# Loading the queries of later batches in two-token runs, so that the score matmuls read them in order

## The chip, the cores and the metric

The kernel runs on one core of one Trainium2 chip. The metric is the device time of one launch in microseconds (us). The kernel before took 751.44 us, the median of three runs that lie between 751.35 and 751.8 us.

## What is computed

For each of 4 batches and 8 heads (576 tokens of 64 numbers, 32 memory slots), a softmax of `phi` over the tokens condenses keys and values into 32 memory keys and 32 memory values. Each query token then attends to those 32 slots. The result, 2304 tokens of 512 numbers, goes through two feed-forward layers, the first with a leaky ReLU, the second with Mish. All data is float32.

```python
a = softmax(phi, over tokens)                          # (b, h, 576, 32)
k_m = einsum('bhsm,bhsd->bhmd', a, k);  v_m = einsum('bhsm,bhsd->bhmd', a, v)
scores = q @ k_m.T / 8                                 # (b, h, 576, 32)
x = softmax(scores, over the 32 slots) @ v_m           # heads side by side: (2304, 512)
h = x @ w_in;   x = maximum(0.01 * h, h) @ w_out       # (2304, 2048) and back
h = x @ w_in2;  out = (h * tanh(softplus(h))) @ w_out2
```

## The kernel before

Every large product is done as three products of TensorE's rounded float32 kind: an operand is split into a rounded part and the rest (`hi` and `lo` in the names). The memory values are first multiplied into `w_in` (`vw_tasks`, L927; matmuls on L947), so that the first layer is computed from the attention weights (`at_t`) directly. The first feed-forward network (`stage1`, L1187) walks over 128 units of 288 tokens by 128 hidden columns: six matmuls on L1198 make a hidden block, ScalarE (ACT) and VectorE (DVE) split it, and twelve matmuls on L1231 add it to four accumulators. Between these units stands the attention of the next batch. The second network (L1552 and L1705) follows.

The attention of batches 1 to 3 is `kv_rest` (L502) and `score_rest` (L676). A batch has two groups `g` of four heads, and each head has its own 32 partitions, so a group's queries fill 128 partitions. One DMA per group loads them: partition `p` of a head gets tokens 18p to 18p+17, one run of 18 tokens of 64 numbers (4,608 bytes). VectorE then transposes the tile in place in blocks of 32 by 32 (L695). After that a partition holds one of 32 features, and along the partition stand token-in-run (18), feature half (2) and partition of origin (32), in this order. Two score blocks follow, one for the even and one for the odd tokens. A block (L709 to L719, the row of its matmuls is L713) has 16 matmuls: two feature halves, four heads, two groups. Each takes 32 rows and gives 32 of the 128 output partitions, over 288 columns. Batch 1 keeps the two groups in two tiles (`qs_t`, `qT_t`), batches 2 and 3 in one (`kvq_t`). VectorE transposes the scores back (L724), the softmax runs over 32 slots, and a last transpose and a split give `at_t`. Batch 0 is done in another way (`score_tasks`, L811: transposes on TensorE, score matmuls on L864), which the change leaves alone.

In the profile a float32 matmul of the program appears as two records, so a score block is 32 records; a matmul on split operands is one.

All instructions are put in order at build time by a planner (`Order.run`, L94): a task has a priority, the engines that may do it with an assumed duration each, and the buffers that it takes. The planner steps through its own clock and places the ready task of lowest priority. SyncE (SP) issues all DMAs, in order, from one queue; an issue waits there until its buffer is free, and those behind it wait too. Where two engines may do a task, L115 takes the one that would end first, after adding a bias; the constant `TOP` is the bias on VectorE for one step (`top`, L371) of unpacking a weight tile (`decode`, L359): ScalarE does it on L374, VectorE on L376.

Of the kernel before, what the change touches and what calls it, by code (L numbers as in the profile page):

```python
# [23 lines left out]
def hop(a, b):  # L24
# [6 lines left out]
K = dict(  # L31
    LAG1=2, WIN=8, OB=2, RS=4, FILL=36, A1=10, S1=8.0,
    A2=30, S2=2.6, V1=2.4, V2=14, W2=56.0, W2S=3.8, O='phi0 kv0 phi1 q0 w0 kv1 q1 w1 w2 w3', HF0=-20.0, HF1=-7.0,
    HFD=0.3, TOP=0.3, HI=0.2, WO=2.0, WOL=1, WC=3.0, WC0=-38.0, V0=3.0, COLD=20, GL=1.5, AL=5.0, XL=22.0, T='0:1 0:1 1:2 0:2 1:2', SB=1,
    DW=280e3, DQ=1.3, DP=1.2, DS=0.78, DI=0.38, L4=0.5, L4P=1.6, L4S=0.8, L4T=5.0, MA=6, QL=4, PL=6, BH=(9,3,3,3,3), FK=-52.5, DWF=0.85, MV="......rvvrrvvrvr",
)

# [122 lines left out]
def kernel(  # L160
# [14 lines left out]
    M = phi.shape[3]  # L175
# [5 lines left out]
    HG = 4  # L181
# [11 lines left out]
    RQ = S // 32  # L193
# [83 lines left out]
    def dma(**args):  # L277
        sched.issued += 1
        nc.sync.dma_start(**args)
# [3 lines left out]
    def add(engines, prio, fn, deps=(), take=(), use=(), bias=None):  # L283
        t = sched.add(engines, prio, fn, deps, take, use, bias)
        for b in (*take, *use):
            if b.pool is spool:
                early.append(t)
            elif b.pool is rawpool:
                middle.append(t)
        return t  # L290


    def dve(n):
        return n / 960 + 0.065
# [4 lines left out]
    def act(n, ps=False):  # L299
        return n / 1196 + (0.051 if ps else 0.093)  # L300
# [4 lines left out]
    def mb(shape_bytes):  # L305
        return shape_bytes / K["DW"]
# [193 lines left out]
    RB = 9  # L500
# [175 lines left out]
    def score_rest(b, pq, ps, dp):  # L676
        qs = [q_s.new([P, RQ, 2, M]), qT_s.new([P, RQ, 2, M])] if b == 1 else [kvq.new([P, NG, RQ, 2, M])] * NG
        q_of = [lambda g=g: qs[g].t if b == 1 else qs[g].t[:, g] for g in range(NG)]
        parts, ld0 = [], None
        for g in range(NG):  # L680
            flat = lambda g=g: q_of[g]().rearrange("p r e i -> p (r e i)")
            new = b == 1 or not g

            def ld(e, g=g, new=new, flat=flat):
                if new:
                    qs[g].make()
                dma(out=flat(), in_=q[b, g * HG:(g + 1) * HG].rearrange("h (p r) d -> (h p) (r d)", r=RQ))

            ld0 = add(
                {"SP": K["DS"] * mb(589824)}, pq - K["QL"], ld, [] if new else [ld0], [qs[g]] if new else [], [] if new else [qs[g]],  # L690
            )
            if b == 1:
                ld0.behind = w_loads[1][K["BH"][3 + g]:][:1]
            parts.append(add(
                {"DVE": dve(1152) + 0.1}, pq + 0.7 * g, lambda e, flat=flat: nc.vector.transpose(out=flat(), in_=flat()), [ld0], (), [qs[g]],  # L695
            ))
        kb = kT[b, 0][0]
        a = [at_tag.new([P, 2, S], F32R) for _ in range(NG)]
        ab = [[], []]
        for hf in range(2):  # L700
            ps0 = ps[hf]
            T = T_tag.new([P, NG, RB, M])
            pss = [misc.new([P, NB1]) for _ in range(NG)]

            def fsc(e, hf=hf, T=T, pss=pss):
                T.make()
                for x in pss:
                    x.make()
                for y in range(2):  # L709
                    for h in range(HG):  # L710
                        for g in range(NG):
                            rows, o = slice(M * h, M * (h + 1)), M * (h ^ g)
                            nc.tensor.matmul(  # L713
                                out=pss[g].t[o:o + M, :].rearrange("p (i r) -> p i r", i=M),
                                lhsT=kb.t[rows, g, y, :],
                                rhs=q_of[g]()[rows].rearrange("p (r u) e i -> p u e i r", u=2)[:, hf, y],
                                start=(y == 0),
                                stop=(y == 1),
                            )  # L719

            ts = add({"PE": 1.2}, ps0, fsc, [*parts, *kT[b, 0][1], *kT[b, 1][1]], [T, *pss], [*qs[:1 + (b == 1)], kb])
            tt = [add(
                {"DVE": dve(NB1)}, ps0 + 0.2,
                lambda e, g=g, T=T, pss=pss: nc.vector.transpose(out=T.t[:, g].rearrange("p r m -> p (r m)"), in_=pss[g].t),  # L724
                [ts], (), [pss[g], T],
            ) for g in range(NG)]
            T3 = lambda T=T: T.t.rearrange("p g r m -> p (g r) m")
            T1 = lambda T=T: T.t.rearrange("p g r m -> p (g r m)")
            n2, N2 = NG * RB, NG * NB1
            sm, sm2 = sm_tag.new([P, n2, 1]), sm_tag.new([P, n2, 1])  # L730
            t1 = add(
                {"DVE": dve(N2)}, ps0 + dp,
                lambda e, T3=T3, sm=sm: nc.vector.tensor_reduce(out=sm.make(), in_=T3(), axis=AX.X, op=ALU.max), tt, [sm], [T],
            )
            t2 = add(
                {"DVE": dve(N2)}, ps0 + 1.5 * dp,
                lambda e, T3=T3, sm=sm: nc.vector.tensor_tensor(out=T3(), in0=T3(), in1=sm.t.to_broadcast([P, n2, M]), op=ALU.subtract),
                [t1], (), [T, sm],
            )
            t3 = add(  # L740
                {"ACT": act(N2)}, ps0 + 2 * dp,
                lambda e, T1=T1: nc.scalar.activation(out=T1(), in_=T1(), func=AF.Exp, scale=0.125), [t2], (), [T],
            )

            def fsum(e, T3=T3, sm2=sm2):
                nc.vector.tensor_reduce(out=sm2.make(), in_=T3(), axis=AX.X, op=ALU.add)
                nc.vector.tensor_scalar(out=sm2.t, in0=sm2.t, scalar1=1e-9, scalar2=None, op0=ALU.add)
                nc.vector.reciprocal(out=sm2.t, in_=sm2.t)

            t4 = add({"DVE": dve(N2) + 0.4}, ps0 + 2.5 * dp, fsum, [t3], [sm2], [T])  # L750
            t5 = add(
                {"DVE": dve(N2)}, ps0 + 3 * dp,
                lambda e, T3=T3, sm2=sm2: nc.vector.tensor_tensor(out=T3(), in0=T3(), in1=sm2.t.to_broadcast([P, n2, M]), op=ALU.mult),
                [t4], (), [T, sm2],
            )
            t6 = add({"DVE": dve(N2)}, ps0 + 3.5 * dp, lambda e, T1=T1: nc.vector.transpose(out=T1(), in_=T1()), [t5], (), [T])
            cols = slice(hf * NB1, (hf + 1) * NB1)
            for g in range(NG):

                def hi(g=g, cols=cols):  # L760
                    if not hasattr(a[g], "t"):
                        a[g].make()
                    return a[g].t[:, 0, cols]

                ab[g].extend(map(keep, hi_lo(
                    ps0 + 4 * dp, NB1, hi, lambda g=g, cols=cols: a[g].t[:, 1, cols], lambda g=g, T=T: T.t[:, g].rearrange("p r m -> p (r m)"),
                    [t6, *ab[g][:1]], [] if hf else [a[g]], [T, a[g]] if hf else [T],
                )))
        for g in range(NG):
            at[b, g] = (a[g], ab[g][0:2], ab[g][2:4])  # L770
# [199 lines left out]
    for x in K["T"].split() + [f"{b}:{NC}" for b in range(2, B)]:  # L970
        b, n_c = map(int, x.split(":"))
# [64 lines left out]
    for g in range(NG):  # L1036
        score_tasks(0, g, -59.5 + 10 * g, (-54.0, K["HF0"]) if not g else (-40.0, K["HF1"]), K["HFD"])
    def next_batch(b):
        d, st = (K["A1"], K["S1"]) if b == 1 else (K["A2"], K["S2"])
        p = base[b] - d  # L1040
        kv_rest(b, p, 0.08 * d / 2)
        score_rest(b, p + 0.1 * d, (p + 0.3 * d, p + 0.3 * d + st), 0.03 * d)
# [42 lines left out]
    for n in range(NM):  # L1085

        kind, u = "io"[n % 2], n // 2
        p = K['W2'] + K['W2S'] * n
# [4 lines left out]
        for j in range(2):  # L1093
            b, ld = bs[j]
# [48 lines left out]
        def save2(e, u=u, wd=wd):  # L1143
# [13 lines left out]
                out=sb.t.rearrange("p a f -> p (a f)").bitcast(F32R), in0=sb.t.rearrange("p a f -> p (a f)"),  # L1157
# [6 lines left out]
            lambda e, u=u, st=st2: dma(out=t_scr[u][0][:, 3:7, 0], in_=st.t.bitcast(F32)), [th, s1], (), [st2],  # L1164
# [3 lines left out]
            lambda e, u=u, sb=sb: dma(out=t_scr[u][0][:, 3:7, 1], in_=sb.t), [tl, s1], (), [sb],  # L1168
# [146 lines left out]
    def place(shape):  # L1315
        at_prio, tag = slots.pop(0)
        return at_prio, tag.new(shape, F32R)
# [63 lines left out]
    for _ in range(4):  # L1381
        b = place([P, 2, 512])[1]
# [223 lines left out]
    rows = [(ob_tag.new([P, DM]), 0) for _ in range(2)]  # L1606
# [206 lines left out]
```

## Time and profile before

| | |
|---|---|
| median of three runs | 751.44 us |
| the profiled execution | 751.76 us, of which the span of its instructions is 749.9 us |
| TensorE matmul busy | 737.7 us (98%) |
| VectorE busy | 546.1 us (73%) |
| ScalarE busy | 404.2 us (54%) |
| DMA | 183.78 MB moved, 245 GB/s over the span |
| granted TensorE clock | 0.997 of full speed, mean of the span |

A matmul's time from start to end overlaps that of its neighbours, so busy time says that TensorE had something in flight, not how fast it went. How fast it went is read from the distance between starts, or from the pieces of the chain of waits, which do not overlap. A row of the profile names a line of the kernel, an engine, an operation, the tile written and the tiles read, and the shape. PE is TensorE, SPq the queue of SyncE that issues DMAs.

### The profile page before, as it was taken

The page shows a single profiled execution, that of the slowest core. Times are in us where ns is not written, and L with a number is a line of the kernel's source. Part 1 is how long each engine was busy: PE and PEld are TensorE (multiplying, and loading weights), DVE is VectorE, ACT ScalarE, POOL GpSimd, SP SyncE. Part 2 cuts the span into 40 slices and gives each one's busy share as a digit, 9 for nine tenths or more (in the row PEclk, how much of TensorE's full clock was granted, in tenths as well). Part 3 has the DMA queues.
Part 4 walks back from the last instruction along what each step waited for, and adds up shares of the span by engine and source line. Part 5 has one row for each costly group of instructions (what it writes and reads, how often), then busy time and mean ns, then how long its engine had stood idle before and what let it go on. Part 6 is the DMA issues. An engine that isn't in the chain of part 4 may idle for free.

```text
span 749.9 us, 16151 instructions
## 1 busy us (share of the span) xinstructions
PE 737.7 (98%) x6167; PEld 699.1 (93%) x6167; DVE 546.1 (73%) x1138; ACT 404.2 (54%) x882; POOL 0.7 (0%) x6
## 2 busy tenths in 40 slices
PE   8899999999999999999999999999999999999997
PEld 7687899968998898999999999999999999999997
DVE  6998859677676866655769798767576965665585
ACT  3876358545464556564466674644455644454443
POOL 0000000000000000000000000000000000000000
PEclk9999999999999999999999999999999999999999
DMA  9882956537869288874278898788987878987466
GB/s 349 308 349 61 349 171 218 182 107 271 280 214 337 76 264 291 273 236 170 99 267 319 330 319 293 227 268 264 301 262 248 265 243 258 292 285 224 126 211 196
DMA packets 90653, 183.78 MB, mean 245 GB/s; under 512 B 7888, under 2 KB 42704, under 8 KB 90576
## 3 DMA queue, kind: packets, MB, share of 16 engines
q1 hardware_dynamic: 90576, 182.75, 72.6%
q8 instruction: 49, 0.80, 0.4%
q14 instruction: 28, 0.23, 0.1%
HBM read 140.25 MB, written 42.47 MB: 244 GB/s over the span
## 4 chain that ended last, share of the span: by engine, by line
PE 96%; DVE 1%; DMA 1%; ACT 1%; issue 0%; SPq 0%
PE acc_t L1231 28%; PE h_t L1552 22%; PE acc_t L1705 17%; PE h_t L1198 13%; PE misc_t L1705 7%; PE misc_t L947 2%; PE acc_t L1552 2%; PE misc_t L713 2%; PE acc_t L484 1%; PE misc_t L622 1%; DMA kvq_t<-in_q_dram 1%; PE acc_t L1029 1%; PE h_t L837 0%; PE misc_t L864 0%; PE misc_t L665 0%
## 5 line engine op out<-in xcount | busy, mean ns | idle before, releaser
L1231 PE MATMUL acc_t<-hi_t,wo_t 128*128 128x288 f32 x1024 | 160.9, 298 | 0.4 <-ACT at_t L310 0.3
L1231 PEld LDWEIGHTS acc_t<-hi_t,wo_t 128*128 128x128 f32 x1024 | 143.5, 188 | 12.5 <-issue 6.7
L1705 PE MATMUL acc_t<-wo_t,hi_t 128*128 128x256 f32 x720 | 133.8, 279 | 0.0
L1198 PE MATMUL h_t<-at_t,vw_t 128*128 128x288 f32 x768 | 124.6, 297 | 2.2 <-ACT at_t L310 0.8
L1212 ACT ACTIVATE hi_t<-h_t 128x288 fp32r<-128x288 f32 x128 | 52.7, 411 | 126.9 <-PE acc_t L1231 112.1
L1705 PEld LDWEIGHTS acc_t<-wo_t,hi_t 128*128 128x128 f32 x720 | 118.1, 188 | 0.2 <-DVE ob_t L312 0.2
L1198 PEld LDWEIGHTS h_t<-at_t,vw_t 128*128 128x128 f32 x768 | 110.1, 190 | 3.1 <-ACT at_t L310 1.1
L1705 PE MATMUL acc_t<-wo_t,lo_t 128*128 128x256 f32 x360 | 102.1, 284 | 0.0
L1219 DVE TENSOR_TENSOR lo_t<-e_t,hi_t 128x288 fp32r<-128x288 f32 x128 | 57.5, 451 | 47.9 <-ACT e_t L1212 23.8
L1231 PE MATMUL acc_t<-lo_t,wo_t 128*128 128x288 f32 x512 | 90.6, 299 | 1.0 <-DVE lo_t L1219 1.0
L1231 PEld LDWEIGHTS acc_t<-lo_t,wo_t 128*128 128x128 f32 x512 | 74.6, 188 | 10.6 <-issue 8.6
L1552 PE MATMUL h_t<-xt_t,vw_t 128*128 128x384 f32 x396 | 79.1, 336 | 0.0
L1674 DVE TENSOR_TENSOR lo_t<-wo_t,hi_t 128x384 fp32r<-128x384 f32 x94 | 52.0, 555 | 36.6 <-ACT hi_t L310 35.3
L1552 PE MATMUL h_t<-xt_t,wo_t 128*128 128x384 f32 x352 | 75.5, 336 | 0.0
L1705 PEld LDWEIGHTS acc_t<-wo_t,lo_t 128*128 128x128 f32 x360 | 67.6, 188 | 0.0
L1552 PEld LDWEIGHTS h_t<-xt_t,vw_t 128*128 128x128 f32 x396 | 66.7, 188 | 0.3 <-DVE wo_t L1571 0.3
L310 ACT ACTIVATE hi_t<-wo_t 128x384 fp32r<-128x384 f32 x83 | 43.4, 523 | 40.8 <-PE acc_t L1705 28.3
L1552 PEld LDWEIGHTS h_t<-xt_t,wo_t 128*128 128x128 f32 x352 | 59.4, 188 | 0.1
L1705 PE MATMUL misc_t<-wo_t,hi_t 128*128 128x256 f32 x288 | 54.0, 279 | 0.0
L1212 ACT ACTIVATE e_t<-h_t 128x288 f32<-128x288 f32 x128 | 52.0, 406 | 0.0
L1674 DVE TENSOR_TENSOR lo_t<-vw_t,hi_t 128x384 fp32r<-128x384 f32 x50 | 27.7, 555 | 25.4 <-ACT hi_t L310 25.2
L1577 ACT ACTIVATE wo_t<-wo_t 128x384 f32<-128x384 f32 x53 | 27.6, 520 | 32.4 <-DVE wo_t L1571 32.2
(242 smaller groups left out, 1057.2 us busy)
## 6 DMA issues: line engine op xcount, KB each, us to landing
wo_t<-tscr SPq DMA_DIRECT2D x168, 256.0 KB, 3.8
vw_t<-wsum SPq DMA_DIRECT2D x32, 512.0 KB, 4.7
win_t<-wscr SPq DMA_DIRECT2D x24, 512.0 KB, 4.5
raw_t<-in_moe_w_in_dram SPq DMA_DIRECT2D x19, 512.0 KB, 7.4
raw_t<-in_moe_w_out_dram SPq DMA_DIRECT2D x17, 512.0 KB, 5.8
wsum<-vw_t SPq DMA_DIRECT2D x16, 512.0 KB, 5.2
wo_t<-wsum SPq DMA_DIRECT2D x16, 512.0 KB, 4.5
tscr<-raw_t SPq DMA_DIRECT2D x9, 512.0 KB, 5.8
```

The source lines that it names most:

```text
L310: nc.scalar.activation(out=o, in_=i, func=AF.Copy)
L484: nc.tensor.matmul(out=acc.t[rows, :].rearrange("p (j d) -> p j d", j=2), lhsT=phv()[rows, r, :], rhs=kv.t[rows, :2304].rearrange("p (j r ...
L713: nc.tensor.matmul(out=pss[g].t[o:o + M, :].rearrange("p (i r) -> p i r", i=M), lhsT=kb.t[rows, g, y, :], rhs=q_of[g]()[rows].rearrange("p ...
L947: nc.tensor.matmul(out=pss[g].t[M * (h ^ g):M * (h ^ g) + M, :], lhsT=vT[b, g][0].t[rows, g, h ^ g if b else h // 2, :], rhs=wbs[g].t[rows ...
L1198: nc.tensor.matmul(out=h.t, lhsT=us[g][0].t[:, wi, j0:j0 + P], rhs=ats[g][0].t[:, ai, cols], start=(n == 0), stop=(n == 3 * NG - 1),)
L1212: nc.scalar.activation(out=o, in_=h.t, func=AF.Prelu, alpha=0.01)
L1219: lambda e: nc.vector.tensor_tensor(out=lb.make(), in0=eb.t, in1=hb.t.bitcast(F32), op=ALU.subtract),
L1231: nc.tensor.matmul(out=ac[kk].t, lhsT=wu[0].t[:, wi, kk * P:(kk + 1) * P], rhs=(hb if src == 0 else lb).t, start=(first and (wi, src) == ( ...
L1552: nc.tensor.matmul(out=h.t, lhsT=w[:, wi, c0:c0 + P], rhs=xp[b, xi].ap()[:, j], start=(first and j == 0 and k3 == 0), stop=(j == 1 and k3 ...
L1577: lambda e: nc.scalar.activation(out=t_of[x](), in_=h.t if h else t_of[x](), func=AF.Mish),
L1674: lambda e, hb=hb, lb=lb, src=src: nc.vector.tensor_tensor(out=lb.make(), in0=src(), in1=hb.t.bitcast(F32), op=ALU.subtract),
L1705: nc.tensor.matmul(out=ac[t].t, lhsT=x.t[:, t * P:(t + 1) * P], rhs=T[:, wi], start=(u == 0 and n3 == 0 and first_of), stop=(u == CH - 1 a ...
```

## The change

Each group's queries are now loaded by four DMAs, one per head, instead of one. A head's 576 tokens are cut into nine stretches of 64; of each stretch partition `p` gets two neighbouring tokens, so a partition receives nine runs of 512 bytes. The order of the 18 tokens along the partition is then (stretch, even or odd). After the transpose, the 288 columns of one score block stand as stretch (9) by partition of origin (32), and that is already the order in which the scores are written: the matmul reads nine runs of 32 neighbouring numbers. Before, column order was partition of origin by token-in-run, so the matmul read its numbers 128 apart (512 bytes), nine of them, then stepped by one. The scores are written to neighbouring places in both kernels, with the same column for the same token. The planner is told that these loads take longer (`DQ`, 1.3, in place of `DS`, 0.78).

The bias `TOP` goes from 0.3 to 0.1, which makes VectorE's handicap for L376 smaller. In the order, VectorE now does 33 of these 64 steps (27 before) and ScalarE 31 (37 before).

```diff
-    HFD=0.3, TOP=0.3, HI=0.2, ...
+    HFD=0.3, TOP=0.1, HI=0.2, ...
...
-                dma(out=flat(), in_=q[b, g * HG:(g + 1) * HG].rearrange("h (p r) d -> (h p) (r d)", r=RQ))
+                for h in range(HG):
+                    dma(
+                        out=flat()[M * h:M * (h + 1)].rearrange("p (j x) -> p j x", j=RB),
+                        in_=q[b, g * HG + h].rearrange("(j p r) d -> p j (r d)", r=2, p=M),
+                    )
 
             ld0 = add(
-                {"SP": K["DS"] * mb(589824)}, pq - K["QL"], ld, ...
+                {"SP": K["DQ"] * mb(589824)}, pq - K["QL"], ld, ...
...
                             nc.tensor.matmul(
-                                out=pss[g].t[o:o + M, :].rearrange("p (i r) -> p i r", i=M),
+                                out=pss[g].t[o:o + M, :].rearrange("p (r i) -> p r i", i=M),
                                 lhsT=kb.t[rows, g, y, :],
-                                rhs=q_of[g]()[rows].rearrange("p (r u) e i -> p u e i r", u=2)[:, hf, y],
+                                rhs=q_of[g]()[rows].rearrange("p (r u) e i -> p u e r i", u=2)[:, hf, y],
```

Lines below the edited load stand four lines later in the new kernel: the query transposes are L699, the score matmuls' row is L717, the score transposes L728, the split of a hidden block L1223, and the matmuls of a unit L1202 and L1235.

On SP, the issues around the queries of batch 1 (`qs_t`, `qT_t`), before:

```order
L279 DMA kvq_t<-in_v_dram 128x2x576
L279 DMA qs_t<-in_q_dram 128x1152
L279 DMA qT_t<-in_q_dram 128x1152
L279 DMA raws_t<-in_moe_w_out_dram 128x1024 x2
L279 DMA raw_t<-in_moe_w_out_dram 128x1024 x2
```

and now:

```order
L279 DMA kvq_t<-in_v_dram 128x2x576
L279 DMA qs_t<-in_q_dram 32x9x128 x4
L279 DMA qT_t<-in_q_dram 32x9x128 x4
L279 DMA raws_t<-in_moe_w_out_dram 128x1024 x2
L279 DMA raw_t<-in_moe_w_out_dram 128x1024 x2
```

Two issues have become eight, at the same place in the queue, ahead of four loads of `w_out`.

On DVE, the stretch from the first query transpose of batch 2 to its first score transposes, before (`vw_t` is the product of memory values and `w_in`, `lo_t` the rest of a hidden block):

```order
L695 STREAM_TRANSPOSE kvq_t<-kvq_t 128x1152
L1219 TENSOR_TENSOR lo_t<-e_t,hi_t 128x288
L695 STREAM_TRANSPOSE kvq_t<-kvq_t 128x1152
L312 CAST vw_t<-misc_t 128x512
L1219 TENSOR_TENSOR lo_t<-e_t,hi_t 128x288
L326 TENSOR_TENSOR vw_t<-misc_t,vw_t 128x512 x2
L1276 TENSOR_TENSOR x_t<-acc_t,x_t 128x288 x4
L1219 TENSOR_TENSOR lo_t<-e_t,hi_t 128x288
L724 STREAM_TRANSPOSE T_t<-misc_t 128x288 x2
```

and now:

```order
L699 STREAM_TRANSPOSE kvq_t<-kvq_t 128x1152
L1223 TENSOR_TENSOR lo_t<-e_t,hi_t 128x288
L312 CAST vw_t<-misc_t 128x512
L1223 TENSOR_TENSOR lo_t<-e_t,hi_t 128x288
L326 TENSOR_TENSOR vw_t<-misc_t,vw_t 128x512 x2
L699 STREAM_TRANSPOSE kvq_t<-kvq_t 128x1152
L1223 TENSOR_TENSOR lo_t<-e_t,hi_t 128x288
L728 STREAM_TRANSPOSE T_t<-misc_t 128x288
L1280 TENSOR_TENSOR x_t<-acc_t,x_t 128x288 x4
```

The second query transpose has moved behind the three instructions on `vw_t`, so it is the last piece of work before the scores.

On PE, from the `vw` matmuls that feed those three instructions to the first score block of batch 2, now:

```order
L951 MATMUL misc_t<-win_t,vTb_t 32x512 x8
L1235 MATMUL acc_t<-lo_t,wo_t 128x288 x4
L1202 MATMUL h_t<-at_t,vw_t 128x288 x6
L1235 MATMUL acc_t<-hi_t,wo_t 128x288 x8
L1235 MATMUL acc_t<-lo_t,wo_t 128x288 x4
L1235 MATMUL acc_t<-hi_t,wo_t 128x288 x8
L717 MATMUL misc_t<-kvq_t,kT_t 32x288 x16
```

Before, the same piece was without the last eight matmuls ahead of the scores, so 22 matmuls of 288 columns stood between the two and now 30 do. From the sums over the memory slots of that batch (L622) to its scores there were 82 and are now 80.

## Rows read from the trace of the kernel before

**Rows 1.** The page's chain of work that ended last, shares by engine.

```profile
PE 96%; DVE 1%; DMA 1%; ACT 1%; issue 0%; SPq 0%
```

**Rows 2.** That chain in time: start us, us, what. Batches 1 and 2.

```profile
66.45 2.09 PE misc_t L713 x32
...
155.01 2.57 PE misc_t L713 x23
```

**Rows 3.** Groups by form: line engine op names shapes xcount | busy us, mean ns | idle.

```profile
L947 PE MATMUL misc_t<-win_t,vTb_t 64*32 64x512 f32 x240 | 16.3, 601 | 0.0
...
L713 PE MATMUL misc_t<-kvq_t,kT_t 32*32 32x288 f32 x128 | 10.6, 778 | 0.0
...
L484 PE MATMUL acc_t<-kvq_t,phi_t 32*32 32x128 f32 x144 | 4.5, 270 | 0.5 <-ACT phi_t L466 0.5
...
L864 PE MATMUL misc_t<-kvq_t,kT_t 64*32 64x288 f32 x16 | 1.4, 415 | 0.0
```

**Rows 4.** PE's timeline, batch 1's scores: start us, us, line op names xcount.

```profile
66.38 0.65 PE L713 MATMUL misc_t<-qs_t,kT_t 32*32 32x288 f32 x1
...
66.86 0.66 PE L713 MATMUL misc_t<-qs_t,kT_t 32*32 32x288 f32 x1
```

**Rows 5.** PE's timeline, one `vw` block, to 26.70 and to 26.90 us.

```profile
26.34 0.66 PE L947 MATMUL acc_t<-win_t,vTb_t 64*32 64x512 f32 x8
...
26.34 1.09 PE L947 MATMUL acc_t<-win_t,vTb_t 64*32 64x512 f32 x16
```

**Rows 6.** The query tensor's instructions: xcount, ns min/median/max, first and last start.

```profile
L279 SPq DMA_DIRECT2D kvq_t<-in_q_dram x5: 333/446/967, 2.6 to 228.8; - x5
```

**Rows 7.** The same view, 141 to 144 us: batch 2's two query loads.

```profile
L279 SPq DMA_DIRECT2D kvq_t<-in_q_dram x2: 333/650/967, 141.9 to 142.2; - x2
...
DMA to landing us min/median/max: 4.3/5.8/7.2
```

**Rows 8.** The DMA view of 36 to 52 us; last number: us from issue to landing.

```profile
DMA packets 2148, 6.39 MB, mean 399 GB/s; under 512 B 176, under 2 KB 176, under 8 KB 2146
...
raws_t<-in_moe_w_out_dram SPq DMA_DIRECT2D x2, 512.0 KB, 12.1
```

**Rows 9.** The DMA view of 228 to 230 us, and the query tensor there.

```profile
DMA packets 575, 0.67 MB, mean 336 GB/s; under 512 B 42, under 2 KB 540, under 8 KB 575
...
DMA to landing us min/median/max: 6.7/6.7/6.7
```

**Rows 10.** PE's timeline, batch 2, from memory sums to first score block.

```profile
139.76 2.11 PE L622 MATMUL misc_t<-kvq_t,phi_t 64*32 64x128 f32 x136
...
150.79 1.09 PE L947 MATMUL misc_t<-win_t,vTb_t 64*32 64x512 f32 x16
...
154.94 2.64 PE L713 MATMUL misc_t<-kvq_t,kT_t 32*32 32x288 f32 x32
```

**Rows 11.** DVE's timeline in the same stretch.

```profile
149.50 1.38 DVE L695 STREAM_TRANSPOSE kvq_t<-kvq_t 128x1152 f32<-128x1152 f32 x1
152.01 0.69 DVE L312 CAST vw_t<-misc_t 128x512 fp32r<-128x512 f32 x1 [1.14 <-PE misc_t L947]
...
153.08 1.28 DVE L326 TENSOR_TENSOR vw_t<-misc_t,vw_t 128x512 fp32r<-128x512 f32 x2
```

**Rows 12.** Timelines of DVE and PE, batch 3's second query transpose and scores.

```profile
235.56 1.38 DVE L695 STREAM_TRANSPOSE kvq_t<-kvq_t 128x1152 f32<-128x1152 f32 x1
...
240.03 2.64 PE L713 MATMUL misc_t<-kvq_t,kT_t 32*32 32x288 f32 x32
```

**Rows 13.** Timelines of SP and ACT: loads behind batch 1's queries, their first use.

```profile
37.60 0.98 SPq L279 DMA_DIRECT2D raws_t<-in_moe_w_out_dram  x2
...
54.19 0.68 ACT L369 ACTIVATE raws_t<-raws_t 128x512 f32<-128x512 f32 x1
```

**Rows 14.** Groups by form, the two ways of the step that `TOP` weighs.

```profile
L374 ACT ACTIVATE raw_t<-raw_t 128x512 int32<-128x512 uint16 x18 | 12.3, 684 | 0.0
...
L376 DVE TENSOR_SCALAR raw_t<-raw_t 128x512 int32<-128x512 int32 x18 | 7.5, 421 | 2.0 <-DMA raw_t<-in_moe_w_in_dram 2.0
```

More of the change, by code (lines that the diff above doesn't have):

```diff
@@ L33 @@
     A2=30, S2=2.6, V1=2.4, V2=14, W2=56.0, W2S=3.8, O='phi0 kv0 phi1 q0 w0 kv1 q1 w1 w2 w3', HF0=-20.0, HF1=-7.0,
-    HFD=0.3, TOP=0.3, HI=0.2, WO=2.0, WOL=1, WC=3.0, WC0=-38.0, V0=3.0, COLD=20, GL=1.5, AL=5.0, XL=22.0, T='0:1 0:1 1:2 0:2 1:2', SB=1,
+    HFD=0.3, TOP=0.1, HI=0.2, WO=2.0, WOL=1, WC=3.0, WC0=-38.0, V0=3.0, COLD=20, GL=1.5, AL=5.0, XL=22.0, T='0:1 0:1 1:2 0:2 1:2', SB=1,
     DW=280e3, DQ=1.3, DP=1.2, DS=0.78, DI=0.38, L4=0.5, L4P=1.6, L4S=0.8, L4T=5.0, MA=6, QL=4, PL=6, BH=(9,3,3,3,3), FK=-52.5, DWF=0.85, MV="......rvvrrvvrvr",
@@ L686, in ld @@
                     qs[g].make()
-                dma(out=flat(), in_=q[b, g * HG:(g + 1) * HG].rearrange("h (p r) d -> (h p) (r d)", r=RQ))
+                for h in range(HG):
[3 more added lines that the diff above has]
+                    )
             ld0 = add(
-                {"SP": K["DS"] * mb(589824)}, pq - K["QL"], ld, [] if new else [ld0], [qs[g]] if new else [], [] if new else [qs[g]],
+                {"SP": K["DQ"] * mb(589824)}, pq - K["QL"], ld, [] if new else [ld0], [qs[g]] if new else [], [] if new else [qs[g]],
             )
```

## The prediction

> **What bounds the kernel now.** I read the chain of work that ended last first: TensorE has 96% of it [rows 1]. So a microsecond taken from a matmul that stands on TensorE's queue after the start-up is a microsecond off the end, as long as nothing new makes TensorE wait. Next I looked in the same chain, in order of time, for the pieces that the change touches. There are six score blocks; batch 1's two have pieces of 2.09 us, the four of batches 2 and 3 pieces of 2.56 to 2.57 us [rows 2]. They make 2 x 2.09 + 4 x 2.57 = 14.5 us of chain.
>
> Then I asked, in the groups by form, how fast these matmuls go beside others of plain float32 [rows 3]. L864 and L947 read neighbouring numbers: 415 ns for 288 columns and 601 ns for 512, so (601 - 415) / 224 = 0.83 ns per column and a remainder of 415 - 239 = 176 ns. A score matmul of batches 2 and 3 takes 778 ns for 288 columns, (778 - 176) / 288 = 2.09 ns per column. In batch 1 the timeline shows the pace directly: eight records start within 0.05 us, the next eight 0.48 us later [rows 4], so 0.48 / 288 = 1.67 ns per column. The score matmuls go at half of L947's pace in batch 1, and at two fifths of it in batches 2 and 3.
>
> Two things set them apart from L947: they read numbers 512 bytes apart, and they use 32 rows of the array instead of 64. L484 settles which one. It has tiles of 32 by 32 too, reads runs of 64 neighbouring numbers, and takes 270 ns for 128 columns; 176 + 128 x 0.83 = 282 [rows 3]. So the small tile does not slow it. Nor does running eight at once: eight records of L947 run together and the next eight start 1.09 - 0.66 = 0.43 us later, 0.84 ns per column [rows 5]. What remains is the stride.
>
> **The matmuls.** A block is four rounds of eight records. Batch 1's 2.09 us are 4 x 0.48 + 0.16 [rows 2, 4]. With runs of 32 neighbours I take the pace of L947 and L864: 4 x 0.239 + 0.16 = 1.12 us. The same formula gives L947's block as 2 x 0.43 + 0.16 = 1.02 us, against 1.09 in the timeline [rows 5], whose pieces run 0.07 longer than the chain's (2.64 against 2.57 [rows 2, 10]). The saving is 2 x (2.09 - 1.12) + 4 x (2.57 - 1.12) = 1.94 + 5.80 = 7.7 us. No row shows runs as short as 32. Bounds: L947's pace (7.7 saved) and the present one (0 saved). I take L947's, since L484's runs of 64 are the nearest row and are not slower than that.
>
> The Trainium skill speaks to this: in "SBUF — State Buffer", section "Door 1: The DMA port swizzle", reads run at full rate when several hit the same 16-byte line, and each step to a new line costs. The trace agrees as far as it goes (2.09 against 0.83 ns per column). By that rule the new form, four numbers to a line, has the full pace, and the first two rivals below would have no chance; the rows alone leave them one.
>
> **The query loads.** Each of six group loads becomes four issues. An issue takes a median of 446 ns on SP [rows 6], so a batch's eight take 3.6 us where batch 2's two took 0.33 and 0.97 [rows 7]: the last one is 2.3 us later, and so is what is queued behind it. The packets shrink from 4,608 to 512 bytes. Large packets (6.39 MB in 2148, 2,975 bytes each) moved at 399 GB/s [rows 8], small ones (1,165 bytes) at 336 GB/s [rows 9]. If a packet has a fixed cost, the difference of 1/336 - 1/399 = 0.00047 us per KB belongs to 0.86 - 0.34 = 0.52 more packets per KB, 0.9 ns each. At 512 bytes, 1.95 packets per KB, I estimate 1 / (0.00298 + 1.09 x 0.0009) = about 250 GB/s. A batch's 1.18 MB then needs 4.7 us instead of 2.95, 1.7 more. Both delays may overlap, so the last query lands 2.3 to 4.0 us later.
>
> Who waits? *Batch 2*: TensorE ends L622 at 141.8 and reaches the scores at 154.94 [rows 10], 13.1 us later; with two matmuls of 0.13 fewer, 12.8. The second transpose, which ended 4.1 us ahead of the scores [rows 11], now stands behind `vw_t`. There are 30 matmuls between L947 and the scores instead of 22, so L947 starts 4.15 + 8 x 0.13 = 5.2 us before them, 7.6 us after L622, and ends at 8.6. VectorE began 0.2 us behind L947 and needed 2.35 us for the cast, a split and two L326 [rows 11]; with the transpose of 1.38 it is done at 12.5. TensorE comes at 12.8: 0.3 us to spare. The last query landed at the latest at 142.2 + 7.2 = 149.4 [rows 7], 7.6 us after L622; 2.3 to 4.0 later is 9.9 to 11.6, and VectorE wants it at 11.15. So TensorE waits 0 to 0.2 us. *Batch 3*: the second load was issued at 228.8 [rows 6] and landed 6.7 us later, at 235.5 [rows 9], just as VectorE transposed it, 3.1 us ahead of the scores [rows 12]. Three more issues (1.3), the slower transfer of one group (0.85) and up to 1.3 behind the first group's issues make it up to 3.45 late: 0 to 0.4 us of waiting. *Batch 1*: the first loads behind the queries were issued from 37.6 and landed 12.1 us later, about 49.7; their first user is at 54.19 [rows 8, 13]. A delay of 2.7 + 1.7 = 4.4 us just fits.
>
> I charge 0.5 us for these waits and for the new order elsewhere, between -0.5 (a reordering can also fill a gap) and 2.
>
> **The bias.** Six shifts go from ScalarE (684 ns) to VectorE (421 ns) [rows 14], the other way from the words "more readily on ScalarE". VectorE gains 2.5 us of work, ScalarE loses 4.1; TensorE's full queue covers both, so 0. Without that cover it would cost the 2.5.
>
> **The sum.** On the profiled execution: 751.76 - 7.7 + 0.5 = 744.5 us. It lay 0.3 above the median of the runs, so 744.2.
>
> **Rivals**, from the median of the runs.
> *Short runs cost.* Each step to a new run of 32 stalls the read: half-way between 0.83 and batch 1's 1.67 ns per column a block is 4 x 0.36 + 0.16 = 1.6, the saving 2 x 0.49 + 4 x 0.97 = 4.9, the time 751.4 - 4.9 + 0.5 = 747.0. For it: no row has runs below 64. Against it: L484.
> *The change doesn't do what it says.* The stride isn't the brake; it is the pair of groups that shares each 32 rows, which the new kernel keeps. Then nothing is saved and the waits stay: 752. For it: of these matmuls only L713's have two tiles on each 32 rows. Against it: L947 puts four on each 64 rows without loss [rows 5], and batches 1 and 2 differ in pace with the same tiling.
> *The loads come too late*, which ends slower. If loads into 32 partitions move slower than estimated, TensorE stands at the scores. With x us of transfer beyond the 2.95, batch 2 waits x - 3.85 (from 7.6 to 11.15, and the 0.3 to spare), batch 3 x / 2 - 1.8 (3.1 to spare, 1.3 used up on SP), and batch 1, given no further slack, x - 4.5. The sum, 2.5 x - 10.15, passes the 7.7 saved at x = 7.1: 1.18 MB in 10.1 us, 117 GB/s. At 90 GB/s x is 10.2, the waits 15.3 and the time 759. For it: batch 1's queries lie in a saturated stretch [rows 8]. Against it: 336 GB/s with packets only twice as large [rows 9].
> *Half pace.* At half of the estimate (125 GB/s, x = 6.5) the waits are 6.1 and the time 749.8, still a little faster.
>
> The Trainium skill has a rule for the last one, in the same section of "SBUF — State Buffer": a transfer into 32 partitions reaches 8 of 16 ports and so half the bandwidth. By it 749.8 would be the time. No row here shows a load into 32 partitions.
>
> **How the numbers follow.** Forecast 72% (743.0 to 746.5); short runs 10% (747.0); half pace 5% (749.8, on the border); no gain 7% (752); loads late beyond the turning point 6% (759). About 0.2% (1.5 us, so 749.9) is what a measurement of this kernel can tell from no change. So faster 0.85, same 0.09, slower 0.06. The range runs from 743.0, where no wait is left and a gap closes, to 749.9, above the partial cases; the last two rivals are left out.
>
> **What would show it.** Right: the score matmuls' mean near 415 ns, blocks of 1.1 us in the chain, all six alike, and no idle time of TensorE ahead of them. Short runs: means between 450 and 650. No gain: 650 to 780 as now. Late loads: idle time of TensorE ahead of L717 that ends on VectorE's query transposes, which themselves wait for the query DMAs. The forecast is wrong if the blocks shrink and the end doesn't follow; then TensorE waits in another place, and the new chain names it.

## The result and the profile after

The changed kernel takes 744.53 us, the median of four runs (743.73 to 745.1); the kernel before, in the same comparison, 751.39 us. The ratio is 0.9907, 95% interval [0.989, 0.9924]: 6.9 us faster. The profiled execution took 745.1 us, its span is 743.3 us.

The chain of work that ended last is TensorE's as it was [rows 1]. First the score blocks in it, all six (start us, us, what):

```profile
67.19 1.13 PE misc_t L717 x32
76.62 1.48 PE misc_t L717 x32
153.45 1.13 PE misc_t L717 x32
157.97 1.13 PE misc_t L717 x32
237.07 1.13 PE misc_t L717 x32
240.77 1.13 PE misc_t L717 x32
```

They answer to the pieces of 2.09 and 2.57 us [rows 2]. Five are alike, whatever the batch, and the second is 0.35 us longer. Together they make 7.1 us of chain, where 14.4 stood (the six pieces of before add up to 14.44). The groups by form show the same for the single matmul, 407 ns where 778 stood [rows 3]:

```profile
L717 PE MATMUL misc_t<-kvq_t,kT_t 32*32 32x288 f32 x128 | 4.8, 407 | 0.0
```

In the timeline of TensorE (PE is the matmul, PEld its weight load) and VectorE, the first two rows are the starts of the first two rounds of batch 1, 0.27 us apart (0.48 before [rows 4]). The other rows are the start of its second block:

```profile
67.12 0.42 PE L717 MATMUL misc_t<-qs_t,kT_t 32*32 32x288 f32 x1
...
67.39 0.40 PE L717 MATMUL misc_t<-qs_t,kT_t 32*32 32x288 f32 x1
...
76.19 0.65 DVE L326 TENSOR_TENSOR vw_t<-misc_t,vw_t 128x512 fp32r<-128x512 f32 x1
...
76.55 0.67 PE L717 MATMUL misc_t<-qs_t,kT_t 32*32 32x288 f32 x2
...
76.90 0.10 PEld L717 LDWEIGHTS misc_t<-qT_t,kT_t 32*32 32x32 f32 x1 [0.22 <-DVE vw_t L326]
```

The first group's matmul starts at 76.55, the second group's only at 76.90. Its score tile is a `misc_t` that VectorE's L326 was still reading until 76.84. That wait of 0.35 us is new and comes from the new order.

A second measure leaves the start-up out, whose length differs from one execution to the next. It runs from the first start of a score matmul to the last start of a matmul of the second network. In the instruction rows of a line, the two numbers ahead of the last semicolon are first and last start. Of before:

```profile
L713 PE MATMUL misc_t<-qs_t,kT_t x32: 648/658/660, 66.4 to 78.2; 32*32 32x288 f32 x32
...
L1705 PE MATMUL acc_t<-wo_t,lo_t x360: 276/285/288, 418.3 to 745.2; 128*128 128x256 f32 x180
```

and of after:

```profile
L717 PE MATMUL misc_t<-qs_t,kT_t x32: 401/401/425, 67.1 to 77.7; 32*32 32x288 f32 x32
...
L1709 PE MATMUL acc_t<-wo_t,lo_t x360: 276/285/285, 411.9 to 738.8; 128*128 128x256 f32 x180
```

Before, this stretch was 745.2 - 66.4 = 678.8 us, now it is 738.8 - 67.1 = 671.7 us: 7.1 less. I call it the stretch below. The start-up went the other way in these two executions, 67.1 us against 66.4. A second profile of the same changed kernel has 65.9 us of start-up and a stretch of 671.8: between these two the start-up differs by more than a microsecond and the stretch by 0.1. The measure is fair only where the same work lies between its two marks, which is so in all kernels below but one.

The query loads of batch 2 in the query tensor's instruction rows (SPq is the issue; the second row is who waited, us and times):

```profile
L279 SPq DMA_DIRECT2D kvq_t<-in_q_dram x8: 333/454/929, 140.6 to 144.4; - x8
...
  DVE kvq_t L699: 1.7, 1
...
DMA to landing us min/median/max: 2.3/2.9/3.4
```

In the timeline, the end of L622, VectorE's transposes and the scores:

```profile
138.35 2.25 PE L622 MATMUL misc_t<-kvq_t,phi_t 64*32 64x128 f32 x144
...
145.47 1.38 DVE L699 STREAM_TRANSPOSE kvq_t<-kvq_t 128x1152 f32<-128x1152 f32 x1 [1.72 <-DMA kvq_t<-in_q_dram]
...
151.65 1.36 DVE L699 STREAM_TRANSPOSE kvq_t<-kvq_t 128x1152 f32<-128x1152 f32 x1
...
153.38 1.20 PE L717 MATMUL misc_t<-kvq_t,kT_t 32*32 32x288 f32 x32
```

VectorE waited 1.7 us for the first group, and no wait of TensorE follows from it. The second transpose ended at 153.01, 0.37 us ahead of the scores. TensorE lists no wait for a query.

### The profile page after: what moved, and what is told of

It is laid out like the page before. It is cut to its first block, busy times and chain, and to the rows that moved or that the text cites. A ratio compares the mean times of both kernels' runs of the same rounds, so it can differ in the third digit from the quotient of the medians.

```text
span 743.3 us, 16194 instructions
## 1 busy us (share of the span) xinstructions
PE 729.6 (98%) x6167; PEld 698.4 (94%) x6167; DVE 547.6 (74%) x1145; ACT 400.5 (54%) x875; POOL 0.7 (0%) x6
## 4 chain that ended last, share of the span: by engine, by line
PE 96%; DVE 2%; ACT 1%; issue 0%; DMA 0%
PE acc_t L1235 28%; PE h_t L1556 22%; PE acc_t L1709 17%; PE h_t L1202 13%; PE misc_t L1709 7%; PE misc_t L951 2%; PE acc_t L1556 2%; PE acc_t L484 1%; PE misc_t L717 1%; PE misc_t L622 1%; PE acc_t L1033 1%; DMA phi_t<-in_phi_dram 0%; PE h_t L841 0%; PE misc_t L868 0%; PE misc_t L665 0%
## 5 line engine op out<-in xcount | busy, mean ns | idle before, releaser
L1235 PE MATMUL acc_t<-hi_t,wo_t 128*128 128x288 f32 x1024 | 160.8, 298 | 0.2 <-DVE x_t L312 0.2
L1235 PEld LDWEIGHTS acc_t<-hi_t,wo_t 128*128 128x128 f32 x1024 | 143.7, 188 | 8.2 <-issue 5.9
L1202 PE MATMUL h_t<-at_t,vw_t 128*128 128x288 f32 x768 | 124.5, 297 | 2.2 <-ACT at_t L310 0.8
L1202 PEld LDWEIGHTS h_t<-at_t,vw_t 128*128 128x128 f32 x768 | 110.0, 190 | 3.4 <-ACT at_t L310 1.1
L1235 PE MATMUL acc_t<-lo_t,wo_t 128*128 128x288 f32 x512 | 90.6, 299 | 1.3 <-DVE lo_t L1223 1.3
L1223 DVE TENSOR_TENSOR lo_t<-e_t,hi_t 128x288 fp32r<-128x288 f32 x128 | 57.2, 451 | 43.9 <-ACT e_t L1216 23.5
L1235 PEld LDWEIGHTS acc_t<-lo_t,wo_t 128*128 128x128 f32 x512 | 74.5, 188 | 10.8 <-issue 9.3
```

Source lines behind the costliest of these rows:

```text
L1202: nc.tensor.matmul(out=h.t, lhsT=us[g][0].t[:, wi, j0:j0 + P], rhs=ats[g][0].t[:, ai, cols], start=(n == 0), stop=(n == 3 * NG - 1),)
L1223: lambda e: nc.vector.tensor_tensor(out=lb.make(), in0=eb.t, in1=hb.t.bitcast(F32), op=ALU.subtract),
L1235: nc.tensor.matmul(out=ac[kk].t, lhsT=wu[0].t[:, wi, kk * P:(kk + 1) * P], rhs=(hb if src == 0 else lb).t, start=(first and (wi, src) == ( ...
```

## The experiments

Four kernels that differ in one part each, compared with the kernel before (751.2 us in that comparison).

**The read alone.** Before, with

```diff
-  out=...rearrange("p (i r) -> p i r", i=M), rhs=...rearrange("p (r u) e i -> p u e i r", u=2)[:, hf, y]
+  out=...rearrange("p (r i) -> p r i", i=M), rhs=...rearrange("p (r u) e i -> p u e r i", u=2)[:, hf, y]
```

> The kernel before with one edit: its score matmuls read the columns as nine runs of 32 neighbours, loads, bias and the order of all instructions unchanged. (The columns of a block then belong to other tokens than the rest of the kernel takes them for.) Theory: the stride of the read is the whole of the gain. Then the score matmuls take 400 to 415 ns, the six blocks 1.13 us each, 7.4 us of chain go, and the time is 751.4 - 7.4 = 744.0 us (743.5 to 744.6). Rival: loads and the new order bring part of the gain; then this kernel stays above 746.

Measured: 743.18 us, ratio 0.9895 [0.9883, 0.9908]; all six blocks 1.13 us, the stretch 736.1 - 64.9 = 671.2 us, 7.6 less than before. The theory holds: the read alone gives the whole gain, with loads, bias and order untouched. The time lies 0.3 us under the stated range, which counted 7.4 us of chain where six blocks of 1.13 make 7.7.

**The read in order, the write strided.** Before, with the read as above and

```diff
-  out=pss[g].t[o:o + M, :].rearrange("p (i r) -> p i r", i=M),
+  out=pss[g].t[o:o + M, :].rearrange("p (i r) -> p r i", i=M),
```

> The kernel before; its score matmuls read nine runs of 32 neighbours and write each run to places nine numbers (36 bytes) apart, which keeps each token in its column with the loads of before. Theory: only the stride of the read brakes, a strided write costs nothing: 744.0 us as in the first, 0.5 us or less under the changed kernel. Rival: a strided write brakes as a strided read did; then the blocks stay near 2.1 to 2.6 us and the time at 750 to 752 (half-way: 747 to 748).

Measured: 744.24 us, ratio 0.9908 [0.9897, 0.992]. By form:

```profile
L713 PE MATMUL misc_t<-kvq_t,kT_t 32*32 32x288 f32 x128 | 4.8, 407 | 0.0
```

The stretch is 737.1 - 66.0 = 671.1 us, as in the first. A write at steps of 36 bytes costs nothing, so the gain is to be had without touching the loads. The profiled executions of the two lie 1.1 us apart (743.63 and 742.5), and so do their start-ups (66.0 and 64.9). The Trainium skill says otherwise ("SBUF — State Buffer", section "Door 1: The DMA port swizzle", in its remark on PSUM's 8-byte lines): any non-contiguous access there slows matmuls significantly. These matmuls write PSUM 36 bytes apart and take 407 ns as the contiguous ones do, so for them the measurement decides against it.

**Loads and order alone.** The changed kernel with the read and write of before.

> The changed kernel with the read and the write of the score matmuls as before (read 512 bytes apart; columns then belong to other tokens): eight loads for two, the changed order and the bias stay. Theory: loads and order cost 0.5 us, so 751.9 us (751.4 to 752.6), and blocks of 2.1 and 2.6 us. Rival: loads and order bring part of the gain: under 750.

Measured: 752.74 us, ratio 1.0018 [1.0006, 1.003]; the stretch 744.8 - 65.2 = 679.6 us, 0.8 more than before. Loads, order and bias together cost something and bring nothing, as the theory said; the time lies 0.1 us above its range. Of the 0.8 us, 0.5 stand in the score blocks, of which batch 1's second now takes 2.54 us in the chain, not 2.09.

**The bias back.** The changed kernel with `TOP=0.3`.

> The changed kernel with the bias TOP back at 0.3. Theory: six shifts more or less on VectorE lie beside TensorE's queue; 744.5 us, within 1 us of the changed kernel. Rival: VectorE's 2.5 us of extra work are on the path in the changed kernel: then this one takes 742.0; or ScalarE's 4.1 us were on it and this one takes up to 748.

Measured: 748.16 us, ratio 0.996 [0.9946, 0.9975] against 0.9907 of the changed kernel. The theory that the bias is without weight fell: without it half of the gain goes. The figure of the second rival, up to 748, was met; whether for its reason is the question of what follows. TensorE's waits from the first scores on (us in total, times, longest), the changed kernel's first:

```profile
PE h_t L1556 <- ACT wo_t L310: 0.6, 1, 0.6
PE acc_t L1235 <- DVE x_t L312: 0.2, 1, 0.2
```

```profile
PE h_t L1556 <- ACT wo_t L310: 1.1, 1, 1.1
PE acc_t L1235 <- DVE x_t L1280: 1.1, 4, 0.4
PE h_t L1556 <- ACT vw_t L310: 0.9, 1, 0.9
```

The stretch is 740.6 - 64.5 = 676.1 us, 4.3 to 4.4 more than the changed kernel's two. But not all of that is loss, since this order puts more work behind the first scores. In these rows of the two stretches (window, us, PE busy and in brackets its matmuls), the changed kernel's first, it has ten matmuls more:

```profile
67.10:738.90 671.80, 671.01 (x5375) 648.12 (x5374) 490.80 (x1012) 356.84 (x782) 0.00 (x0) 1.00 0.73 243
```

```profile
64.50:740.70 676.20, 673.12 (x5385) 649.79 (x5384) 489.19 (x1005) 361.75 (x797) 0.00 (x0) 1.00 0.73 242
```

At 0.13 us each (44 of L1235 take 5.82 us in the chain) they make 1.3 us, which this kernel does not spend ahead of the scores; the other kernels have the changed one's number. For equal work the stretch is 674.8, so 3.0 to 3.1 us are lost. The listed waits make 2.3 of that: TensorE stands for VectorE's sums of `x_t`, which the order puts just ahead of its need, and for ScalarE's roundings in the second network. The score blocks make 0.2. Where the other 0.5 us lie was not found. ScalarE's work as such is not the cause, since the kernel before has as much of it (404.2 us busy against 404.7).

So the next comparison asked whether the bias is worth something by itself, or only with the order that the new load price `DQ` brings. (The 2.5 us that its first expectation puts in the second network are not all waits: of these there are 2.0 us there, against 0.6 in the changed kernel.) Before took 751.43 us in it.

**The bias alone.** Before, with `TOP=0.1`.

> The kernel before with the bias TOP at 0.1 alone. Putting the bias back cost the changed kernel 3.6 us, 2.5 of it in the second network, where TensorE waited 2.0 us in all for weights that ScalarE rounds. Theory: that is a matter of the order which the planner happens to find; before's order has no such waits beyond 0.6 us, so the bias has nothing to take away there: 751.2 us (750.2 to 752.2). Rival: the lighter ScalarE is worth 2.5 to 3.6 us in any order: 747.6 to 748.7.

Measured: 751.07 us, ratio 0.9993 [0.9983, 1.0003]; the stretch 745.4 - 67.2 = 678.2 us, 0.6 less. By the times the bias alone is within what can be told from no change, and far from the rival's 2.5. The 0.6 us of the stretch have a place: before, TensorE waits 0.6 us for `wo_t` in the second network (L1552), and here it does not.

**Strided writes with the new bias.** The second kernel with `TOP=0.1`.

> The kernel with strided writes (loads as before, reads of neighbours) and TOP at 0.1. Theory: the bias is nothing in itself: 744.2 us (743.2 to 745.2). Rival: it takes 2.5 us or more off: 740.6 to 741.7, faster than the changed kernel by 3 us.

Measured: 743.14 us, ratio 0.9888 [0.9871, 0.9905]; the stretch 736.2 - 65.7 = 670.5 us, 0.6 less than with the old bias, as in the experiment before. From the first scores on TensorE waits 0.5 us in all in it; with the old bias it waits 1.1, and the 0.6 for `wo_t` are again what goes. The time lies 0.1 us under the range of the theory.

**New loads in the old order.** The changed kernel's loads, read and write, with price and bias of before:

```diff
-  {"SP": K["DQ"] * mb(589824)}, pq - K["QL"], ld, ...        # TOP=0.1
+  {"SP": K["DS"] * mb(589824)}, pq - K["QL"], ld, ...        # TOP=0.3
```

> The changed kernel's loads, read and write with before's load price and bias, so that TensorE, VectorE and ScalarE keep before's order. Theory: the score blocks give 7.4 us and the eight loads per batch cost 0 to 0.5 us where the order leaves them time; in this order the second transpose of batch 2 stands ahead of the vw work, so VectorE may wait for the last query and hand up to 1.5 us on to TensorE: 743.8 to 745.5 us. Rival: the order is what makes the loads bearable: above 747.

Measured: 743.23 us, ratio 0.989 [0.9874, 0.9906]; the stretch 737.2 - 66.0 = 671.2 us. That is within 0.1 of the two kernels with the loads of before: eight loads per batch cost this kernel nothing. The time is 0.6 us under the stated range, and the wait that the theory feared for VectorE's first transpose did not reach TensorE.

**The changed kernel again**, beside these three.

> The changed kernel as it is, beside the others on the same chip: 744.5 us (743.7 to 745.1) by its first runs.

Measured: 744.33 us, ratio 0.9906 [0.989, 0.9921], so 1.1 us behind the one with the old order, though the intervals overlap; the stretch, 737.7 - 65.9 = 671.8 us, is 0.6 longer. Its chain has the 1.48 us block once more; the other order has six of 1.13.

**The old price with the new bias.** The changed kernel with `DS` for `DQ` alone.

> The changed kernel with the planner's price of the query loads back at DS (0.78), all else as changed, bias 0.1 included. It is the fourth of the four pairings of price and bias with the new loads and reads; three took 748.2 us (new price, old bias), 744.3 (both new) and 743.2 (both old). Theory: only the order that comes out counts, and this is the order of the kernel with strided writes and the new bias, 743.1 us, to which the loads add 0.1: 743.2 us (742.4 to 744.0), and 670.6 us from the first score matmul to the last one of the second network. Rival: the planner needs the longer price so that the loads come in time: 745 or more, with TensorE waiting at the scores of batch 2 or 3.

Measured: 742.81 us, ratio 0.9878 [0.9862, 0.9895]; the stretch 736.0 - 65.5 = 670.5 us. TensorE's waits from the first scores on:

```profile
PE acc_t L1235 <- ACT at_t L310: 0.3, 1, 0.3
PE acc_t L1235 <- DVE x_t L312: 0.2, 1, 0.2
```

The wait of 0.6 us for `wo_t` is gone, and none came at the scores. The four pairings of price and bias, all with new loads and new read, by their stretch:

| | bias 0.3 | bias 0.1 |
|---|---|---|
| price `DS` | 671.2 | 670.5 |
| price `DQ` | 676.1 (674.8 for equal work) | 671.7, 671.8 |

For equal work the longer price costs 3.6 us with the old bias and 1.2 with the new one. (The whole times of the two kernels with the old bias, 748.16 and 743.23, are 4.9 apart; they come from two comparisons and have the start-up in them.) The bias repairs an order that the price had spoilt. This last kernel is ahead of the other three; its distance to the changed one is 1.2 us by the stretch, while the intervals of the two ratios overlap.

Two kernels, one execution each, ask what it is in the stride that brakes. Each gives the score matmuls of the kernel before other patterns to read.

**Steps.**

> The kernel before, its score matmuls reading 288 numbers of their tile at other steps (scores then of other tokens). Batch 1: neighbours and every 2nd (first block), every 4th and every 8th (second). Batch 2 the same again. Batch 3: every 16th, 32nd (first block), 64th, 128th (second); feature half 0 has the first of each pair, half 1 the second. Read from the timeline as the distance between rounds of eight records. Theory A: a number at a new 16-byte place costs a step each; then 1, 2 and 4 differ (0.24 us a round for neighbours, up to 0.48 to 0.6 from 4 on, in between for 2) and 4 to 128 are all alike. Theory B: only large steps brake (512 bytes): all rounds up to every 32nd at 0.24 us, and 128 alone at 0.48 to 0.6.

Measured, from TensorE's timeline of batch 1, the first record of each round of eight:

```profile
66.23 0.42 PE L731 MATMUL misc_t<-qs_t,kT_t 32*32 32x288 f32 x1
...
66.49 0.40 PE L731 MATMUL misc_t<-qs_t,kT_t 32*32 32x288 f32 x1
...
66.73 0.41 PE L731 MATMUL misc_t<-qs_t,kT_t 32*32 32x288 f32 x1
...
66.99 0.41 PE L731 MATMUL misc_t<-qs_t,kT_t 32*32 32x288 f32 x1
...
75.66 0.67 PE L731 MATMUL misc_t<-qs_t,kT_t 32*32 32x288 f32 x1
...
76.15 0.68 PE L731 MATMUL misc_t<-qs_t,kT_t 32*32 32x288 f32 x1
...
76.66 0.69 PE L731 MATMUL misc_t<-qs_t,kT_t 32*32 32x288 f32 x1
...
77.18 0.69 PE L731 MATMUL misc_t<-qs_t,kT_t 32*32 32x288 f32 x1
```

Neighbours go at 0.26 and 0.24 us a round, every 2nd number at 0.26, every 4th and 8th at 0.49 to 0.52. Theory A holds in its main point, but every 2nd number is not in between: it is as fast as neighbours. Batch 2, with both groups in one tile, gives the same blocks in the chain as batch 1 (1.15 and 2.19 us). In batch 3, also in one tile, the step does matter: the block at steps of 16 and 32 takes 2.44 us and that at 64 and 128 takes 2.68. The next kernel bears on why.

**Runs and shifts.**

> The kernel before, its score matmuls reading in other patterns (scores then of other tokens). Batch 1: every 16th, 32nd (first block), 64th, 128th (second), the groups in two tiles. Batch 2: runs of 2, 4 (first block), 8 and 16 neighbours (second), each run 512 bytes behind the last. Batch 3: the old read, the second group shifted against the first by 0 and 128 bytes (first block), 256 and 64 bytes (second). By the rule of 16-byte places runs of 4 and more have the full pace (0.24 us a round) and runs of 2 about half of the loss; if each change of run stalls, runs of 8 and 16 are still slower than 0.24. Batch 3: if the two groups of a row of tiles hinder each other because their addresses fall together, a shift brings the round from 0.60 to batch 1's 0.48 us; if not, all four stay at 0.60.

Measured: batch 1's rounds at steps of 16, 32, 64 and 128 numbers are all 0.47 to 0.49 us apart. So from 16 bytes on, the size of the step is without effect there. Batch 2's two blocks (runs of 2 and 4, then of 8 and 16):

```profile
153.93 1.32 PE L735 MATMUL misc_t<-kvq_t,kT_t 32*32 32x288 f32 x32
...
156.97 1.20 PE L735 MATMUL misc_t<-kvq_t,kT_t 32*32 32x288 f32 x32
```

Runs of 8 and 16 give the 1.20 us of the changed kernel (153.38 above), so a change of run costs nothing from 8 on. Of the first block the half with runs of 2 is slower, and the half with runs of 4 is not, which shows in the instruction rows of its two halves (x of the second also holds the end of the first; ns min/median/max):

```profile
L735 PE MATMUL misc_t<-kvq_t,kT_t x16: 452/470/482, 153.9 to 154.3; 32*32 32x288 f32 x16
...
L735 PE MATMUL misc_t<-kvq_t,kT_t x24: 398/402/466, 154.2 to 154.9; 32*32 32x288 f32 x24
```

and the same view of batch 3's first block, old read, groups shifted against each other by 0 and then by 128 bytes:

```profile
L735 PE MATMUL misc_t<-kvq_t,kT_t x16: 753/778/804, 236.3 to 236.9; 32*32 32x288 f32 x16
...
L735 PE MATMUL misc_t<-kvq_t,kT_t x24: 658/668/804, 236.8 to 238.0; 32*32 32x288 f32 x24
```

A shift by 128 bytes brings the matmul from 778 to 668 ns, close to batch 1's 658. The other block, shifted by 256 and then by 64 bytes, has the same two medians in that order: 256 bytes do not help, 64 do.

**Four loads with long runs.** Before, with each group loaded by four DMAs of one head, runs of 4,608 bytes.

> The kernel before, each group's queries by four loads of 32 partitions with the old runs of 4,608 bytes. It tells whether 32 partitions or the short packets slow the loads: batch 2's queries take 4.3 to 7.2 us to land in the kernel before. By the rule that 32 partitions get half the bandwidth a load of 147 KB at 125 to 200 GB/s, one after the other, takes 5.9 to 9.4 us for a batch; with four loads side by side in the queue all ports are busy and it is 3 to 4 us. Time: 751.2 us (750.2 to 753).

Measured: one time of 751.27 us, the stretch 744.9 - 66.0 = 678.9 us, as before. Batch 2's loads:

```profile
L279 SPq DMA_DIRECT2D kvq_t<-in_q_dram x8: 332/420/767, 141.5 to 145.0; - x8
...
DMA to landing us min/median/max: 2.3/3.1/3.6
```

They land as those with 512-byte runs do (2.3/2.9/3.4). Short packets did not slow these loads of batch 2; for batch 1 see the next section.

## Why the prediction was right, point by point

**TensorE as the bound: right.** The score blocks gave 14.4 - 7.1 = 7.3 us and the stretch 7.1: what left the chain left the time.

**The pace of the matmuls: right.** A block was to take 1.12 us and takes 1.13; the 7.7 us are 7.6 where nothing else changes (the read alone). The reason was the stride, and that holds: the rival that short runs cost was excluded by runs of 4, 8 and 16. By the Trainium skill (the same section of "SBUF — State Buffer") two hits in a 16-byte line are needed for full rate. The traces agree in part: with every 2nd number, so two in a line, the pace was full (0.26 us a round), and one in a line halved it (0.49 to 0.52). But runs of 2, also two in a line, took 470 ns where runs of 4 took 402, so two were not always enough.

**What the prediction left open** is why batches 2 and 3 were slower than batch 1 at the same stride (2.09 against 1.67 ns per column). The rival of the pair of groups was partly right: the two groups of a row of tiles do hinder each other at the distances of before, 4,608 bytes, and at 256 more. Shifted by 64 or 128 bytes, they run as in batch 1. The stride is the larger part, and reading neighbours removes both.

**The query loads: right in the end, wrong in two terms.** The step "the last query lands 2.3 to 4.0 us later" failed. Batch 2's last load was issued at 144.4 and landed at most 3.4 us later, by 147.8, 7.2 us after the end of L622 (138.35 + 2.25); before it was 7.6 [rows 7, 10]. The last issue did come later, 3.8 us after that end where it had been 0.4. But a load of 147 KB lands in 2.3 to 3.4 us, and the eight move while the next are issued; the two large ones took 4.3 and 7.2. The two delays that I added do not stack. At the 125 GB/s of the half-pace rival the 1.18 MB would have needed 9.4 us, and they were all there at most 7.2 us after the first issue, at 164 GB/s or more with the latency in it.

The rival's rule is another matter than its price. While batch 1's queries moved, in a stretch in which the DMA engines were busy throughout, the rate fell. These are the windows of 46 to 48 us (the last two numbers are the DMA engines' busy share and GB/s) of the kernel before, of the four loads with long runs, and of the changed kernel:

```profile
46.00:48.00 2.00, 2.00 (x23) 1.98 (x16) 2.00 (x5) 1.21 (x3) 0.00 (x0) 1.00 1.03 420
```

```profile
46.00:48.00 2.00, 2.00 (x15) 2.00 (x16) 2.00 (x5) 1.31 (x3) 0.00 (x0) 1.00 1.04 233
```

```profile
46.00:48.00 2.00, 2.00 (x22) 1.94 (x15) 2.00 (x5) 1.17 (x3) 0.00 (x0) 1.00 1.21 200
```

Four loads of 32 partitions for one of 128 brought the rate from 420 to 233 GB/s, and short runs to 200. So the second term that failed is the estimate of 250 GB/s: it charged the short packets alone, and the larger part of the loss comes without them. By the Trainium skill (again section "Door 1: The DMA port swizzle" of "SBUF — State Buffer") a transfer into 32 partitions reaches half of the ports and so gets half the bandwidth. The trace agrees at batch 1 (233 against 420), though these loads are also smaller, and a load by itself was not tried. The kernel had slack for it: by the prediction's own sums 200 GB/s, x = 2.95, makes no batch wait.

VectorE's part was right: 0.3 us to spare were forecast, 0.37 measured. At batch 1 the two `raws_t` loads behind the queries were issued 8.6 us later than before, 46.2 against 37.6 [rows 13], since an issue there took up to 1.5 us and SyncE stood 2.9 us ahead of the last one until an earlier load (`kvq_t` from `in_v_dram`) had landed. The instruction rows of that tile behind the queries:

```profile
L279 SPq DMA_DIRECT2D raws_t<-in_moe_w_out_dram x2: 352/440/527, 46.2 to 47.0; - x2
L369 ACT ACTIVATE raws_t<-raws_t x2: 672/679/686, 55.9 to 56.4; 128x512 f32<-128x512 f32 x2
...
DMA to landing us min/median/max: 6.5/6.8/7.0
```

They landed in 6.8 us where it had been 12.1 [rows 8]. The second was there by 47.0 + 7.0 = 54.0, before by 38.1 + 12.5 = 50.6: 3.4 us later against the 4.4 forecast, and ScalarE first used them at 55.9. That this is near is luck, since the parts were not as forecast: the issue came 8.6 us later, not 2.7, and the way was 5.3 us shorter, not 1.7 longer.

**The 0.5 us for waits and order: right in size, in another place.** No query was waited for. 0.35 us stand at the second block of batch 1 behind L326, and the stretch is 0.5 to 0.6 longer than in the old order.

**The bias at 0: nearly right from before, wrong within the change.** By itself it is 0.6 us of gain by the stretch, one wait for `wo_t`, which the times cannot tell from nothing. But in the order that the new price makes it is worth 3.1. The step that failed is "TensorE's full queue covers both, so 0". The prediction reasoned about VectorE's and ScalarE's sums of work under TensorE's queue, and the effect came through the order: who stands just ahead of a need. So the prediction did not see two large terms, +3.6 for the price and -3.1 for the bias. They nearly cancelled, and the 0.5 that it charged is what was left of them: that part of the agreement is luck.

## What to carry to other kernels

In these float32 matmuls (32 by 32 tiles, 288 columns) a moving operand, the one that is streamed through the array, lost half of its pace when it was read at steps of 16 bytes or more (0.47 to 0.52 us a round against 0.24 to 0.27), and two matmuls on the same rows added to it by their addresses. Reading neighbours and writing 36 bytes apart instead was free, so try to permute on the way out before changing a load. When a planner sets the order, try each of its constants with and without the edit: here a higher price for a load cost 3.6 us, and a bias that looked like part of the improvement mostly mended that. To compare variants whose start-up scatters, measure between two instructions behind it, and count that the same work lies between them.

## What the runs showed that I had not expected

The start-up. Of the profiles of these kernels some show TensorE's granted clock at 0.83 as the mean of 30 to 40 us, one at 0.66 and others at 1.00, for kernels with much the same work there; the clock's two levels are 1.2 and 2.4 GHz, so 0.83 is a mixture of both. Windows of the changed kernel and of the one with the old order (first column the window, then PE busy; PEclk is third from the end):

```profile
20.00:30.00 10.00, 8.07 (x82) 5.36 (x80) 9.12 (x27) 8.37 (x18) 0.00 (x0) 1.00 1.03 407
30.00:40.00 10.00, 7.28 (x40) 6.81 (x41) 9.85 (x24) 8.98 (x21) 0.00 (x0) 0.83 0.60 213
```

```profile
20.00:30.00 10.00, 9.03 (x129) 6.33 (x117) 8.67 (x25) 8.73 (x18) 0.00 (x0) 1.00 1.03 403
30.00:40.00 10.00, 5.86 (x34) 4.75 (x35) 9.79 (x25) 9.32 (x22) 0.00 (x0) 1.00 0.55 190
```

TensorE was the busier in the 10 us ahead in the second. But the kernel with the read alone also kept 1.00, with 8.04 us busy in the same 10, so that does not settle it. Start-ups with the same work in them range from 64.9 to 67.2 us over these profiles: 64.9 to 66.0 where that mean is 1.00, 65.9 to 67.2 where it is 0.83, and 65.4 where it is 0.66. So the clock alone does not sort them, and what sets them was not tried.
